# Moving the start addresses of an attention, mixture-of-experts and feed-forward kernel's SBUF pools to multiples of 512 bytes

## The chip, the cores and the metric

The kernel runs on one core of one Trainium2 chip. The metric is the time of the program on the device in microseconds (us), the median of three runs; lower is better. PE is TensorE, DVE is VectorE, ACT is ScalarE, POOL is GpSimd, SP is SyncE, whose queue issues the plain DMAs. SBUF is the memory that the engines read operands from: 128 partitions, in each of which a tile takes a run of bytes. An address below is the byte in a partition at which a tile or a pool of tiles starts.

## The reference, cut to what matters

```python
# q, k, v: (8, 8, 576, 64); attention inside chunks of 64 positions
scores = scale * q_c @ k_c^T; attn = softmax(scores); x = (attn @ v_c) as (4608, 512)
# mixture of experts: 8 experts, each token goes to the one with the largest logit
logits = x @ w_gate; e = argmax(logits); gate = softmax(logits)[e]
x = gate * (relu(x @ w1[e]) @ w2[e])              # w1 512x1024, w2 1024x512
# feed-forward with a rational activation
h = x @ w_in                                      # 512x2048
g = (a0 + a1*h + a2*h^2 + a3*h^3) / (1 + |b0|*|h| + |b1|*h^2 + 1e-6)
return g @ w_out                                  # 2048x512, float64 weights
```

## The kernel before

**Numbers.** Every large product is made from two parts of each operand, a high part in fp32r (the value as TensorE's single-pass format keeps it) and a low part, the rest. `mm3` issues three matmuls for one product: high with high, high with low, low with high (`PASSES`). `split` makes the parts of a weight: ACT copies the raw tile to the high part, DVE (GpSimd for the feed-forward weights that come late) subtracts it for the low part.

**Stages.** First comes attention in 36 tiles of 128 tokens, ordered by hand on PE. It writes x to memory, computes the routing, and sorts tokens into slots. Then come eight experts, each on 512 gathered tokens (the first on 384), ordered by hand on PE, DVE and ACT. `Expert.first(c)` makes 12 matmuls into `h` (stationary: w1, moving: the transposed tokens `xT`), `Expert.second(c)` 12 matmuls into four accumulators `y` (stationary: `hT`, moving: w2). Between them run the extra tiles of 128 tokens (`Extra`, tiles with an `s` or `r` in their names: `hs`, `ys`, `hr`, `yr`), which pass through the same products with their own copies of the weights (`s1`, `s2`) as the moving operand. Last comes the feed-forward in 9 blocks of 512 tokens and 16 chunks c of 128 hidden columns: `first(b, c)` makes the product `f` (stationary: the weights `wf`, moving: `yT`) and the activation on ACT and DVE into `g`; `second(b, c)` makes `z` (stationary: `g`, moving: `wf`). Each is 12 matmuls of 512 columns per chunk. The order inside this last stage is the planner's.

**Where tiles stand.** Pools are laid one after the other from the low end of SBUF in the order in which they are opened; a tile's bytes are rounded up to 32. In front of the first stand 16,384 bytes set aside and four constants of 32. `const` holds small tiles (ident, gate, index tables), 2,976 bytes in all. `xg_p` holds, beside its three buffers of 2,048 bytes, five small tiles of 32 bytes for the extra tiles' indices (`if`, `ix` twice, `ct`, `ce`). Worked out from these sizes:

| pool | what it holds | start before | past a multiple of 512 | start after | past a multiple of 512 |
|---|---|---|---|---|---|
| const | ident and small tables | 16,512 | 128 | 16,512 | 128 |
| ring_a | weights of expert 0, extra tiles' weights, `wf` for c 8 to 15 | 19,488 | 32 | 19,968 | 0 |
| tmp | raw weights, activation's t and u | 85,024 | 32 | 85,504 | 0 |
| xg_p | gathered tokens | 101,408 | 32 | 101,888 | 0 |
| h_p | `hT`, `g` and the extra tiles' `xTs`, `hTs` | 107,712 | 192 | 108,032 | 0 |
| xt_a | `xT`, `yT` of even number | 120,000 | 192 | 120,320 | 0 |
| ring_b | weights of experts 1 to 7, `wf` for c 0 to 7; before it, attention's pools | 136,384 | 192 | 136,704 | 0 |
| xt_b | `xT`, `yT` of odd number | 201,920 | 192 | 202,240 | 0 |
| o_p, cv_p | outputs; conversion of the last weights | 218,304; 222,400 | 192 | 218,624; 222,720 | 0 |

Inside these pools every operand of a 512-column matmul stands a multiple of 512 bytes from its pool's start. Pools opened from the high end (`once`, `rt_p`, `a3_p`) don't move. `ring_b`, `xt_b`, `o_p` and `cv_p` are opened over tiles of earlier stages with `reuse_waits="tile"`: a new tile waits for the old ones whose bytes it takes.

The lines that the text speaks of: L136 and L137 (`split`), L253 (transposes), L259 (`mm3`), L440 to L459 (the activation in `first`), L550 and L569 (attention's q and k).

Of the kernel before, what the change touches and what calls it, by code (L numbers as in the profile page):

```python
# [9 lines left out]
F32 = mybir.dt.float32  # L10
F32R = mybir.dt.float32r
BF16 = mybir.dt.bfloat16
I32 = mybir.dt.int32
U32 = mybir.dt.uint32
# [18 lines left out]
PASSES = ((0, 0), (0, 1), (1, 0))  # L33
CW = 256
CQ = 1.0 + 1e-6
MAN = {mybir.EngineType.PE, mybir.EngineType.DVE, mybir.EngineType.Activation}
SIGN = -0x80000000
EXP_BIAS = 893.0 * 2.0 ** 20
# [3 lines left out]
def kernel(  # L42
# [22 lines left out]
    slots = dram.tile([NE * NT, 1], U32, name="slots")  # L65

    const = ctx.enter_context(tc.tile_pool(name="const", bufs=1))
    ring = {"A": ctx.enter_context(tc.tile_pool(name="ring_a", bufs=8))}
    tmp = ctx.enter_context(tc.tile_pool(name="tmp", bufs=4))

    xg_p = ctx.enter_context(tc.tile_pool(name="xg_p", bufs=3))
# [11 lines left out]
    a3_p = rctx.enter_context(tc.tile_pool(name="a3_p", bufs=2, side="right"))  # L83


    ident = const.tile([128, 128], F32, name="ident")
    make_identity(nc, ident)
    ones = once.tile([128, 128], BF16, name="ones")
    nc.gpsimd.memset(ones, 1.0)
# [32 lines left out]
    cq = const.tile([128, 1], F32, name="cq")  # L122
    nc.vector.memset(cq, CQ)

# [150 lines left out]
    def load_extra(e, nm):  # L275
        r = []
        for src, lab, deint in ((w1r, "w1", True), (w2r, "w2", False)):
            r.append([load_w(extra_src(src, e, c), "A", f"{lab}{nm}_{c}", deint, alternate(c))
                      for c in range(4)])
        return r  # L280

    def expert_of(k_ap):
        return nc.values_load(k_ap, engines=[mybir.EngineType.SP], min_val=0, max_val=NE - 1,
                              skip_runtime_bounds_check_because="one expert's index, or 0, "
                              "out of a table made by comparisons")

    def extra_idx(t, nm):
        m = o_p.tile([128, NE * NOVF], F32, tag="o", name=f"m{nm}")
        V.scalar_tensor_tensor(m, cidx, t[:, 0:1], stf, op0=ALU.is_equal, op1=ALU.mult)
        f = xg_p.tile([128, 2], F32, tag="if", name=f"if{nm}", bufs=1)  # L290
        V.tensor_reduce(f[:, 0:1], m, axis=AX.X, op=ALU.add)
        V.tensor_tensor(out=f[:, 0:1], in0=f[:, 0:1], in1=t[:, 1:2], op=ALU.add)
        V.tensor_scalar(f[:, 1:2], f[:, 0:1], float(NT - 1), None, op0=ALU.min)
        idx = xg_p.tile([128, 2], U32, tag="ix", name=f"ix{nm}", bufs=2)
        V.tensor_copy(idx, f)
        return idx

# [135 lines left out]
    def first(b, c):  # L433
# [13 lines left out]
        last_act = nc.scalar.activation(r, r, AF.Square).ins  # L447
        V.scalar_tensor_tensor(qq, qq, CQ, r, op0=ALU.add, op1=ALU.mult)  # L448
        V.scalar_tensor_tensor(qq, qq, -2.0, r, op0=ALU.add, op1=ALU.mult)  # L449
# [34 lines left out]
    with man:  # L484
# [373 lines left out]
        man.close()  # L858
        man.enter_context(tc.manual_schedule(engines=MAN))

# [65 lines left out]
        def small(name, shape, dt=F32):  # L926
            return rt_p.tile([128] + shape, dt, name=name)
# [44 lines left out]
        ce = small("ce", [NE])  # L972
# [51 lines left out]
        def next_extra(e):  # L1024
            return Extra(extra_idx(tab[:, e], f"s{e}"), (ws1[e], ws2[e]), f"s{e}")
# [223 lines left out]
                               skip_runtime_bounds_check_because="a sum of tile counts over all "  # L1249
                               "tokens, raised to NSTAT, is within these bounds")  # L1250
        with tc.For_i(NSTAT, n_end, 1) as kk:
            ct = xg_p.tile([128, 2], F32, tag="ct", name="ct", bufs=1)
            nc.vector.tensor_copy(ct, tab[:, ds(kk, 1), :].rearrange("p a b -> p (a b)"))
            ce_t = xg_p.tile([1, 1], I32, tag="ce", name="ce_t", bufs=1)
            nc.vector.tensor_copy(ce_t, etab[0:1, ds(kk, 1)])
            ex = Extra(extra_idx(ct, "d"), load_extra(expert_of(ce_t), "d"), "d")
            ex.g()
            ex.x()
            for n in range(2):
                ex.h(n)  # L1260
                ex.r(n)
                ex.t(n)
            for n in range(2):
                ex.y(n)
            ex.out()
# [57 lines left out]
```

## Time and profile before

| what | value |
|---|---|
| median of 3 runs | 1543.64 us (1542.76 to 1545.02) |
| the profiled execution | 1549.44 us, its span 1547.7 us |
| PE busy | 1471.6 us, 95% of the span |
| DVE, ACT, POOL busy | 1284.8, 927.2, 376.8 us |
| granted TensorE clock, mean | 0.990 |

The profile is one execution. Its span is the time from the first to the last instruction. The busy time of PE counts each matmul from its start to its modelled end, and matmuls overlap, so the pace of PE is read from starts: the time from one start to the next. A row that merges n matmuls in the chain of work gives n times that pace; in the timeline a row's length has the last matmul's whole duration in it, so there the pace is taken from the starts of two rows that follow each other.

### The profile page before, as it was taken

What the parts mean: (1) busy time and instruction counts of PE and PEld (TensorE: products, weight loads), DVE (VectorE), ACT (ScalarE), POOL (GpSimd) and SP (SyncE); (2) the same over time, 40 slices, a digit from 0 to 9 for tenths busy, and PEclk for the clock granted to TensorE, in tenths of its full rate; (3) what the DMA queues carried; (4) which work ended last, traced back from release to release, by engine and by line L of the source; (5) the groups of instructions that cost most, each with busy time, mean ns of one, the idle gap of its engine ahead of it and who ended that gap; (6) DMA issues with size and microseconds to landing.
All of it is one profiled execution on the core that took longest, in us unless ns stands there. A gap on an engine that the chain in (4) does not pass through costs nothing.

```text
span 1547.7 us, 22303 instructions
## 1 busy us (share of the span) xinstructions
PE 1471.6 (95%) x7812; PEld 1198.5 (77%) x7812; DVE 1284.8 (83%) x2405; ACT 927.2 (60%) x1456; POOL 376.8 (24%) x307
## 2 busy tenths in 40 slices
PE   6897889999999999997989999999999999999998
PEld 5776678887787777885778888888888888888886
DVE  6787857799889898985989888888888888888886
ACT  5676635454444444444767666666666766766665
POOL 2111122121211212102542222222222222222232
PEclk9999999999999999999999999999999999999999
DMA  8998625777777778663201000010100001000000
GB/s 181 228 251 229 201 84 181 241 248 249 253 233 254 229 232 270 222 214 119 86 28 55 1 28 21 0 48 8 41 14 28 28 1 48 7 35 1 28 1 28
DMA packets 143377, 180.07 MB, mean 116 GB/s; under 512 B 51616, under 2 KB 96672, under 8 KB 143264
## 3 DMA queue, kind: packets, MB, share of 16 engines
q1 hardware_dynamic: 135712, 157.64, 34.1%
q0 software_dynamic: 7552, 21.00, 3.9%
q8 instruction: 62, 1.02, 0.3%
q14 instruction: 51, 0.42, 0.1%
HBM read 140.68 MB, written 37.91 MB: 115 GB/s over the span
## 4 chain that ended last, share of the span: by engine, by line
PE 46%; DVE 3%; issue 2%; POOL 1%; ACT 1%; DMA 0%; SPq 0%; ACTq 0%; POOLq 0%
PE z L259 23%; PE f L259 23%; PE ytp L253 1%; POOL g L459 1%; DVE t L449 1%; POOL wf L137 1%; DVE t L448 0%; DVE t L444 0%; DVE t L450 0%; DMA yg<-ys 0%; DVE t L446 0%; ACT u L445 0%; ACT t L440 0%; DVE yg L718 0%; DVE t L443 0%
## 5 line engine op out<-in xcount | busy, mean ns | idle before, releaser
L259 PE MATMUL f<-yT,wf 128*128 128x512 f32 x1728 | 419.4, 394 | 5.7 <-DVE t L446 2.2
L259 PE MATMUL z<-wf,g 128*128 128x512 f32 x1680 | 411.1, 395 | 9.0 <-ACT g L458 4.6
L259 PEld LDWEIGHTS f<-yT,wf 128*128 128x128 f32 x1728 | 323.5, 188 | 80.5 <-DVE t L446 3.1
L259 PEld LDWEIGHTS z<-wf,g 128*128 128x128 f32 x1680 | 314.6, 189 | 82.1 <-POOL g L459 6.0
L459 POOL TENSOR_TENSOR g<-t,g 128x512 fp32r<-128x512 f32 x140 | 209.6, 1498 | 531.8 <-ACT g L458 501.3
L259 PE MATMUL h<-xT,w 128*128 128x512 f32 (+1 forms) x768 | 184.7, 390 | 6.4 <-DVE hT L379 6.4
L259 PE MATMUL y<-w,hT 128*128 128x512 f32 x744 | 184.0, 396 | 0.0
L443 DVE TENSOR_TENSOR t<-t,f 128x512 f32<-128x512 f32 x144 | 98.6, 685 | 100.6 <-ACT u L442 100.2
L259 PEld LDWEIGHTS h<-xT,w 128*128 128x128 f32 x768 | 144.0, 190 | 35.7 <-DVE hT L379 8.1
L444 DVE SCALAR_TENSOR_TENSOR t<-t,co,u 128x512 f32<-128x512 f32 x144 | 159.1, 1105 | 0.0
L259 PEld LDWEIGHTS y<-w,hT 128*128 128x128 f32 x744 | 136.9, 188 | 28.2 <-issue 0.4
L445 ACT ACTIVATE u<-t,cq 128x512 f32<-128x512 f32 x144 | 104.5, 726 | 85.9 <-DVE t L444 85.3
L458 ACT ACTIVATE g<-t 128x512 fp32r<-128x512 f32 x140 | 89.0, 636 | 99.5 <-DVE t L450 99.5
L440 ACT ACTIVATE t<-f,co 128x512 f32<-128x512 f32 x144 | 112.1, 778 | 49.4 <-PE f L259 34.2
L378 ACT ACTIVATE hT<-h 128x512 fp32r<-128x512 f32 (+1 forms) x64 | 37.5, 585 | 147.0 <-PE h L259 114.1
L450 DVE SCALAR_TENSOR_TENSOR t<-t,co 128x512 f32<-128x512 f32 x144 | 121.8, 846 | 2.0
L448 DVE SCALAR_TENSOR_TENSOR t<-t,u 128x512 f32<-128x512 f32 x144 | 101.9, 708 | 15.5 <-ACT u L447 15.5
L449 DVE SCALAR_TENSOR_TENSOR t<-t,u 128x512 f32<-128x512 f32 x144 | 109.7, 762 | 0.5
L442 ACT ACTIVATE u<-f,co 128x512 f32<-128x512 f32 x144 | 98.3, 683 | 15.0 <-DVE t L449 10.9
L446 DVE SCALAR_TENSOR_TENSOR t<-t,co,f 128x512 f32<-128x512 f32 x144 | 106.2, 738 | 0.0
L447 ACT ACTIVATE u<-u 128x512 f32<-128x512 f32 x144 | 90.4, 628 | 2.2
L441 ACT ACTIVATE t<-f 128x512 f32<-128x512 f32 x144 | 85.1, 591 | 0.0
(203 smaller groups left out, 1951.2 us busy)
## 6 DMA issues: line engine op xcount, KB each, us to landing
raw_w<-in_moe_w_dram SPq DMA_DIRECT2D x64, 512.0 KB
raw_s<-in_moe_w_dram SPq DMA_DIRECT2D x64, 512.0 KB
v<-in_v_dram SPq DMA_DIRECT2D x144, 64.0 KB
xs<-x SPq DMA_DIRECT2D x36, 256.0 KB
out_dram<-o SPq DMA_DIRECT2D x36, 256.0 KB
raw<-in_moe_w_in_dram SPq DMA_DIRECT2D x32, 256.0 KB
raw<-in_moe_w_out_dram SPq DMA_DIRECT2D x32, 256.0 KB
yg<-ys SPq DMA_DIRECT2D x32, 256.0 KB
```

What stands on the lines that cost most here:

```text
L259: nc.tensor.matmul(o, lhsT=lhs(x), rhs=rhs(y), start=(first and n == 0), stop=(last and n == 2))
L440: nc.scalar.activation(p, hp, AF.Identity, scale=a3, bias=a2)
L442: nc.scalar.activation(vv, hp, AF.Abs, scale=b0)
L443: V.tensor_tensor(out=p, in0=p, in1=hp, op=ALU.mult)
L444: V.scalar_tensor_tensor(qq, qq, b1, vv, op0=ALU.mult, op1=ALU.add)
L445: nc.scalar.activation(r, qq, AF.Abs_reciprocal_sqrt, bias=cq)
L446: V.scalar_tensor_tensor(p, p, a1, hp, op0=ALU.add, op1=ALU.mult)
L447: last_act = nc.scalar.activation(r, r, AF.Square).ins
L448: V.scalar_tensor_tensor(qq, qq, CQ, r, op0=ALU.add, op1=ALU.mult)
L449: V.scalar_tensor_tensor(qq, qq, -2.0, r, op0=ALU.add, op1=ALU.mult)
L450: V.scalar_tensor_tensor(p, p, a0, qq, op0=ALU.add, op1=ALU.mult)
L459: nc.gpsimd.tensor_tensor(out=gt[:, 1], in0=p, in1=gt[:, 0].bitcast(F32), op=ALU.subtract)
```

## The change

A new pool `small_p` is opened behind `const` and takes the five small tiles out of `xg_p`. The tile of `ident` gets 80 columns more, which nothing reads. So the tiles that begin behind `const` and `small_p` move up by 480 bytes (`ring_a`, `tmp`, `xg_p`) or 320 bytes (the rest) and begin at multiples of 512. No instruction is added or taken away.

```diff
+PAD = 80
...
     const = ctx.enter_context(tc.tile_pool(name="const", bufs=1))
+    small_p = ctx.enter_context(tc.tile_pool(name="small_p", bufs=1))
     ring = {"A": ctx.enter_context(tc.tile_pool(name="ring_a", bufs=8))}
...
-    ident = const.tile([128, 128], F32, name="ident")
+    ident = const.tile([128, 128 + PAD], F32, name="ident")[:, 0:128]
...
-        f = xg_p.tile([128, 2], F32, tag="if", name=f"if{nm}", bufs=1)
+        f = small_p.tile([128, 2], F32, tag="if", name=f"if{nm}", bufs=1)
...
-        idx = xg_p.tile([128, 2], U32, tag="ix", name=f"ix{nm}", bufs=2)
+        idx = small_p.tile([128, 2], U32, tag="ix", name=f"ix{nm}", bufs=2)
...
-            ct = xg_p.tile([128, 2], F32, tag="ct", name="ct", bufs=1)
+            ct = small_p.tile([128, 2], F32, tag="ct", name="ct", bufs=1)
...
-            ce_t = xg_p.tile([1, 1], I32, tag="ce", name="ce_t", bufs=1)
+            ce_t = small_p.tile([1, 1], I32, tag="ce", name="ce_t", bufs=1)
```

## Rows read from the trace of the kernel before

**Rows 1.** The page's first part: the span, then busy us, share and instructions.
```profile
span 1547.7 us, 22303 instructions
PE 1471.6 (95%) x7812; PEld 1198.5 (77%) x7812; DVE 1284.8 (83%) x2405; ACT 927.2 (60%) x1456; POOL 376.8 (24%) x307
```

**Rows 2.** Windows: busy time and count of each engine by stage, clock, DMA share.
```profile
core 0: us, PE busy (x) PEld busy (x) DVE busy (x) ACT busy (x) POOL busy (x), PEclk, DMA share, GB/s
20.00:160.00 140.00, 118.63 (x1388) 99.77 (x1389) 107.19 (x381) 93.40 (x156) 21.28 (x22) 0.95 0.94 233
280.00:700.00 420.00, 409.55 (x1853) 332.14 (x1852) 377.10 (x775) 191.47 (x249) 75.32 (x65) 0.99 0.75 240
...
840.00:1520.00 680.00, 680.00 (x2995) 554.01 (x2994) 572.97 (x790) 467.65 (x767) 180.72 (x122) 1.00 0.06 19
```

**Rows 3.** The page's chain of work that ended last: shares of the span by engine.
```profile
PE 46%; DVE 3%; issue 2%; POOL 1%; ACT 1%; DMA 0%; SPq 0%; ACTq 0%; POOLq 0%
```

**Rows 4.** Groups of PE's matmuls of 512 columns by tile, with their counts.
```profile
L259 PE MATMUL f<-yT,wf 128*128 128x512 f32 x1728 | 419.4, 394 | 5.7 <-DVE t L446 2.2 <-issue 2.0 <-ACTq L1251 0.9
L259 PE MATMUL z<-wf,g 128*128 128x512 f32 x1680 | 411.1, 395 | 9.0 <-ACT g L458 4.6 <-POOL g L459 4.3
...
L259 PE MATMUL y<-w,hT 128*128 128x512 f32 x744 | 184.0, 396 | 0.0
L259 PE MATMUL h<-xT,w 128*128 128x512 f32 x672 | 166.3, 397 | 6.4 <-DVE hT L379 6.4
...
L259 PE MATMUL ys<-s,hTs 128*128 128x512 f32 x192 | 47.9, 398 | 0.0
L259 PE MATMUL hs<-s,xTs 128*128 128x512 f32 x192 | 47.9, 399 | 0.0
```

**Rows 5.** The chain in order of time, blocks 3 to 5: start, length, matmuls.
```profile
1059.03 5.61 PE z L259 x24
1064.64 5.61 PE f L259 x24
...
1087.05 5.48 PE f L259 x24
...
1098.14 6.16 PE f L259 x27
...
1110.20 0.44 PE ytp L253 x4
...
1138.12 5.48 PE z L259 x24
...
1188.56 6.16 PE f L259 x27
```

**Rows 6.** PE's timeline in the experts' stage: start, length, matmuls merged.
```profile
563.82 2.88 PE L259 MATMUL h<-xT,w 128*128 128x512 f32 x12
566.54 0.60 PE L253 MATMUL xtp<-ident,xg 128*128 128x128 f32 x4
...
573.06 2.98 PE L259 MATMUL hs<-s,xTs 128*128 128x512 f32 x12
575.87 2.92 PE L259 MATMUL y<-w,hT 128*128 128x512 f32 x12
```

**Rows 7.** PE's timeline at expert 0, whose first product has 384 columns.
```profile
235.79 2.25 PE L259 MATMUL h<-xT,w 128*128 128x384 f32 x12
237.88 2.26 PE L259 MATMUL y<-w,hT 128*128 128x512 f32 x9
239.98 2.28 PE L259 MATMUL h<-xT,w 128*128 128x384 f32 x12
```

**Rows 8.** DVE's groups of the low part's subtraction, by ring of the weights.
```profile
L137 DVE TENSOR_TENSOR w<-raw_w,w 128x1024 fp32r<-128x1024 f32 x64 | 78.1, 1220 | 1.7 <-ACT w L136 1.7
L137 DVE TENSOR_TENSOR s<-raw_s,s 128x1024 fp32r<-128x1024 f32 x64 | 77.9, 1218 | 5.5 <-ACT s L136 5.4
```

**Rows 9.** Waits from 20 to 200 us that ended with a load of q or k.
```profile
ACT qkr L550 <- DMA k<-in_k_dram: 9.0, 3, 4.9
```

## The prediction

> **What bounds the kernel now.** I read the page's busy times first. PE is busy for 1471.6 of 1547.7 us, and DVE comes next with 1284.8 [rows 1]. The windows by stage show where that holds: in the feed-forward, from 840 to 1520 us, PE is busy for all of 680 us with 2,995 matmuls, at a granted clock of 1.00, the level of 2.4 GHz; in the experts, from 280 to 700 us, for 409.6 of 420 us. DVE has 573 of 680 and 377 of 420 us there, so it could follow a PE that is a few per cent faster. Attention, from 20 to 160 us, is no PE stage: 118.6 of 140 us, and its DMA engines are at 0.94 [rows 2]. The chain that ended last agrees: of the stretch that it covers nearly all is PE, and DVE, ACT and DMA hold some per cent together [rows 3]. So in the two long stages a nanosecond taken off each matmul comes off the end, and nothing else does.
>
> **What the change does.** It adds, removes and moves no instruction. It changes addresses. The table of pools ahead of this text says which: everything behind the constants goes to a multiple of 512. So I ask whether the trace of before already shows instructions of one shape, in one stage, at different addresses. It does. The feed-forward weights for c 0 to 7 stand in ring_b (192 past a multiple of 512, so a multiple of 64) and those for c 8 to 15 in ring_a (32 past, not a multiple of 64), while `yT` and `g` always stand 192 past. The matmuls of a half differ in nothing else.
>
> **The price of an address on PE.** No matmul of f or z is missing from the trace, so the n-th of the program is the n-th there, and each row of the chain can be told by its chunk. The rows at 1059.03 (z, c 8 and 9) and 1064.64 (f, c 12 to 14) use ring_a: 5.61 / 24 = 233.8 ns from start to start. The rows at 1087.05 and 1098.14 (f, c 0 to 4 of the next block) and at 1138.12 (z, c 6 and 7) use ring_b: 5.48 / 24 = 228.3 and 6.16 / 27 = 228.1 ns [rows 5]. The difference is 5.6 ns, the same for weights that are stationary (f) and for weights that move (z). The experts repeat it: `h`, with w1 from ring_b, goes from 563.82 to 566.54 in 12 matmuls, 226.7 ns each; `hs`, whose weights come from ring_a, from 573.06 to 575.87, 234.2 ns [rows 6]. I take 5.6 ns, the smaller of the two differences. After the change ring_a and its partners stand alike, as ring_b and its partners do today.
>
> One row speaks against so simple a rule. Expert 0's first product has its stationary weights in ring_a too, with 384 columns: from 235.79 to 237.88 is 2.09 us for 12, 174.2 ns each [rows 7]. Against the 226.7 ns of 512 columns in `h` that is 52.5 ns for 128 columns, and 4 x 52.5 = 210, so some 17 ns of each matmul don't go with its columns, in either case: this one seems to pay nothing for its address. I count nothing for these 96.
>
> **How many matmuls gain.** Half of the feed-forward's: of f's 1,728 that is 864, and of z's 1,680 (and 48 more under the name g_last) also 864 [rows 4]. Some of block 0's and of the last block's are covered by ACT and DVE, before 840 us and behind 1515; I take off 88 and keep 1,640. At 5.6 ns they give 9.2 us. In the experts: 192 of `hs` and 192 of `ys` [rows 4], 48 of the first extra tile (hr, yr: 24 each) and 72 of expert 0's second product, whose weights are in ring_a. These are 504, or 2.8 us; with PE at 97.5% there I keep 2.6. The sum is 11.8, so **12 us**. PE's pace there falls by 2.4% in half of the time, and DVE's share rises from 84% to some 86% in the feed-forward, so no other engine becomes the bound.
>
> **What I cost at nothing.** DVE: the subtraction takes 1218 ns when it writes ring_a and 1220 ns when it writes mostly ring_b [rows 8], so phase does not show; bound 0 to 0.2%. Transposes: four of `ytp`, whose source is in xg_p (32 past), take 0.44 us in the chain, 110 ns each [rows 5]; their pace is set by something else or not at all by phase, so I take 0; if 5.6 ns were hidden in each of `ytp`'s 144 (36 tiles of four) it would be 0.8 us. The new pool: the five small tiles keep their numbers of buffers and so their waits. The reused pools: o_p and cv_p now cover 320 bytes more of rt_p's tables, which were last read before those pools open; cover gone, it would be one wait of under a microsecond. DMA: loads of q and k land 192 past a multiple today. The trace doesn't show what an even landing would save, but ACT waits for them for 9.0 us in all [rows 9], so the bounds are 0 and 9; I take 0, since the other engines' shares in attention (DVE 107 of 140 us [rows 2]) close up behind any such gain.
>
> **The rivals.** First, *more than this* (B): even operands at 192 past may pay for not standing at 0. The trace has no large matmul at a multiple of 512, so the bound is the part that doesn't go with the columns, some 17 ns [rows 6, 7], over 5,304 matmuls of 512 columns, 90 us. A quarter of it would be 22 us more: 1510. Against it: the part is the same for 384 columns with other addresses, which looks like a cost of each matmul. The Trainium skill, in "TensorE: Matmul & The Clock Gate", section "Back-to-back issue gap", gives N / 2.4 + 2.5 ns for a warm stream, so 216 ns for 512 columns; by that some 11 ns are open here, but the page says nothing of addresses, and no run here shows 216.
>
> Second, *no change* (C): ring_a's matmuls are slower for where the ring lies, 19 to 85 KB against 136 to 202 KB, or for how far it is from its partner, and 480 bytes alter neither. For it: the 384-column row, which has ring_a and no price. Then the time stays at 1543.6. The Trainium skill, in "SBUF — State Buffer", section "Specifications", speaks for this side: it gives lines of 16 bytes, and every pool of before begins at a multiple of 32, so by it there is nothing to straighten. The trace doesn't agree with that as the whole story: 233.8 against 228.1 ns [rows 5].
>
> Third, *slower* (D): all streams of PE and of ACT begin at one phase and collide. The place is ring_b's matmuls, 864 + 864 + 672 of h and 672 of y, 3,072; the price, if they all fall to 233.8 ns, is 17 us, with nothing gained on ring_a: 1561. It decides from the point at which ring_b's rows pass 231 ns. Against it: today both operands of these matmuls are at one phase, 192, and they are the fast ones.
>
> **How the numbers follow.** The profiled execution took 1549.44 us, 5.8 over the median, span and 1.7 us around it; the difference of 12 us is taken from the median: 1543.6 - 12 = 1531.6, and a profile of about 1537. Chances: this case 0.64, with its own range 1526 to 1538 (5.6 ns could be 3 to 8); B 0.16; C 0.13; D and a planner's order that comes out worse 0.07. Below 1526 is B; I hold its small half, to 1506, inside. Upwards the range goes to 1541, where the gain would be lost in what a measurement of this kernel can tell from no change, 0.2% or 3.1 us. So 1506 to 1541. Faster is this case and B, 0.80; same is C, 0.13; slower 0.07.
>
> **What would show it.** Right: chain rows of 24 matmuls at 5.44 to 5.50 us in both halves of a block, `hs` and `ys` at 227 to 229 ns, a block of the feed-forward of some 89.3 us where it is 90.4 (1098.14 to 1188.56 [rows 5]), and DVE's durations as they were. B would show as rows under 5.40 us in ring_b's half. C would show as rows of 5.61 left where ring_a is read; D as rows of 5.6 where ring_b is. If attention ends some microseconds earlier, the landing of DMAs counts after all. The prediction is wrong if the pace depends on something other than the phase of the two operands, or if the planner orders the feed-forward differently once addresses change.

## The result, and the profile after

The kernel after takes 1529.22 us (median of 4 runs, 1525.02 to 1529.83), the kernel before, measured beside it, 1544.33 us (4 runs, 1542.76 to 1547.04): a ratio of 0.9895, with a 95% interval of 0.9872 to 0.9917. That is 16 us less (0.0105 x 1544), with an interval of 13 to 20. The profiled execution of after took 1525.02 us, the fastest of its four; that of before [rows 1], 1549.44 us, lay 5.1 us over the median just given. So the spans differ by 24.4 us, more than the medians do, and sums below are set against the ratio.

The page's first part, after (it answers [rows 1]):
```profile
span 1523.3 us, 22302 instructions
PE 1454.1 (95%) x7812; PEld 1198.0 (79%) x7812; DVE 1285.5 (84%) x2405; ACT 923.8 (61%) x1456; POOL 376.8 (25%) x307
```
PE has the same 7,812 matmuls and is busy 17.5 us less; DVE's time has not moved. Every engine's instructions stand in the order of before, but for two neighbouring matmuls of attention, so places in the two traces can be matched one to one. All lines behind the constants are 4 further down: L259 is now L263.

The groups by tile, PE's matmuls h and f, give where the stages begin (min, median, max duration, then first and last start). Before:
```profile
L259 PE MATMUL h<-xT,w x768: 335/389/632, 217.6 to 685.3; 128*128 128x512 f32 x168, 128*128 128x384 f32 x24
L259 PE MATMUL f<-yT,wf x1728: 387/393/505, 710.8 to 1527.3; 128*128 128x512 f32 x192
```
After:
```profile
L263 PE MATMUL h<-xT,w x768: 333/389/792, 204.4 to 672.7; 128*128 128x512 f32 x168, 128*128 128x384 f32 x24
L263 PE MATMUL f<-yT,wf x1728: 387/389/628, 697.6 to 1502.8; 128*128 128x512 f32 x192
```
Attention, up to the first h, takes 217.6 and then 204.4 us (13.2 less in these two executions, which differ more than the medians; their granted clock differed there too, 0.88 from 20 to 60 us before and 0.96 after). The experts, from the first h to the first f, take 493.2 and 493.2. The feed-forward, from the first f to the span's end, takes 836.9 and then 825.7: 11.2 us less.

The chain in order of time, after, for one block (it answers [rows 5]; start, length, matmuls):
```profile
1080.27 6.12 PE f L263 x27
...
1088.66 3.40 PE z L263 x15
...
1097.09 2.72 PE z L263 x12
...
1120.11 5.44 PE z L263 x24
1125.55 5.67 PE f L263 x25
1131.22 5.44 PE z L263 x24
1136.66 5.44 PE f L263 x24
...
1169.30 6.12 PE f L263 x27
```
The rows that read ring_a (1131.22, z; 1136.66, f) and those that read ring_b (1120.11) have one pace now: 5.44 / 24 = 226.7 ns. The block goes from 1080.27 to 1169.30, 89.03 us where it was 90.42.

Two more rows of before, from the same view, show what I had not read there:
```profile
1106.57 3.40 PE z L259 x15
...
1114.99 2.72 PE z L259 x12
```
These use ring_b too and already ran at 3.40 / 15 = 226.7 ns. The ring_b rows of [rows 5], 228 ns, each stand right behind a run that read ring_a, and their first matmuls still carry its cost.

The experts' timeline after (it answers [rows 6]):
```profile
560.42 2.88 PE L263 MATMUL hs<-s,xTs 128*128 128x512 f32 x12
563.14 2.89 PE L263 MATMUL y<-w,hT 128*128 128x512 f32 x12
```
From start to start, `hs` takes 2.72 / 12 = 226.7 ns; it was 234.2. Yet the stage is no shorter. The waits of PE in its 487 us (engine, line, what it waited for, us in total, times, longest) show where this went; before, from 223 to 710 us, and after, from 210 to 697:
```profile
PE h L259 <- DVE hT L379: 6.4, 4, 1.8
```
```profile
PE h L263 <- DVE hT L383: 8.9, 4, 2.6
```
The windows of the same two stretches (us, PE busy, PEld, DVE, ACT, POOL, clock, DMA share, GB/s):
```profile
223.00:710.00 487.00, 475.13 (x2197) 387.03 (x2195) 421.83 (x886) 223.32 (x296) 93.22 (x81) 0.99 0.72 230
```
```profile
210.00:697.00 487.00, 472.14 (x2195) 386.82 (x2195) 421.40 (x885) 223.06 (x297) 93.50 (x81) 0.99 0.72 230
```
PE's busy time fell by 3.0 us, and 2.5 us of it came back as a longer wait for `hT` from DVE.

In attention the DMA engines are less busy for what they move. Windows from 60 to 140 us, before and after:
```profile
60.00:140.00 80.00, 71.27 (x855) 59.69 (x851) 66.17 (x240) 56.40 (x94) 15.32 (x16) 0.98 0.96 251
```
```profile
60.00:140.00 80.00, 69.62 (x847) 59.45 (x845) 67.48 (x247) 57.68 (x96) 13.42 (x14) 0.98 0.88 245
```
They moved 251 / 0.96 = 261 GB/s for each unit of busy share before, and 245 / 0.88 = 278 after.

### The profile page after: what moved, and what is told of

Its sections match the earlier page's. It is cut to its first block, busy times and chain, and to the rows that moved or that the text cites. A ratio compares the mean times of both kernels' runs of the same rounds, so it can differ in the third digit from the quotient of the medians.

```text
span 1523.3 us, 22302 instructions
## 1 busy us (share of the span) xinstructions
PE 1454.1 (95%) x7812; PEld 1198.0 (79%) x7812; DVE 1285.5 (84%) x2405; ACT 923.8 (61%) x1456; POOL 376.8 (25%) x307
## 5 line engine op out<-in xcount | busy, mean ns | idle before, releaser
L263 PE MATMUL f<-yT,wf 128*128 128x512 f32 x1728 | 414.6, 392 | 5.7 <-DVE t L450 2.2
L263 PE MATMUL z<-wf,g 128*128 128x512 f32 x1680 | 405.7, 392 | 7.7 <-POOL g L463 4.8
L263 PEld LDWEIGHTS f<-yT,wf 128*128 128x128 f32 x1728 | 324.3, 188 | 75.0 <-DVE t L450 3.1
L263 PEld LDWEIGHTS z<-wf,g 128*128 128x128 f32 x1680 | 314.5, 188 | 75.8 <-POOL g L463 6.7
L263 PE MATMUL h<-xT,w 128*128 128x512 f32 (+1 forms) x768 | 184.7, 390 | 8.9 <-DVE hT L383 8.9
L263 PE MATMUL y<-w,hT 128*128 128x512 f32 x744 | 183.9, 395 | 0.0
L447 DVE TENSOR_TENSOR t<-t,f 128x512 f32<-128x512 f32 x144 | 98.5, 684 | 90.4 <-ACT u L446 89.8
L263 PEld LDWEIGHTS h<-xT,w 128*128 128x128 f32 x768 | 144.2, 191 | 38.0 <-DVE hT L383 10.8
L263 PEld LDWEIGHTS y<-w,hT 128*128 128x128 f32 x744 | 136.9, 188 | 27.9 <-issue 0.4
L444 ACT ACTIVATE t<-f,co 128x512 f32<-128x512 f32 x144 | 112.0, 778 | 33.6 <-PE f L263 17.5
```

The source lines that it names most:

```text
L263: nc.tensor.matmul(o, lhsT=lhs(x), rhs=rhs(y), start=(first and n == 0), stop=(last and n == 2))
L444: nc.scalar.activation(p, hp, AF.Identity, scale=a3, bias=a2)
L447: V.tensor_tensor(out=p, in0=p, in1=hp, op=ALU.mult)
```

## The experiments

**The questions.** My theory was that the two operands of a matmul must stand at one phase, whichever it is, so that their distance decides. Its rival: each operand must by itself begin at a round address. A second pair is about attention: are its loads cheaper for where they land, or is the difference only one between two executions? A third: what swallowed the experts' gain? In the table, "distance" is that of ring_a from the operands that its matmuls are paired with, "landing" is where attention's tiles begin past a multiple of 512, the row is a chain row of 24 matmuls of z that read ring_a, the block goes from the first f of block 4 to that of block 5, and the last column is GB/s over DMA share from 60 to 140 us, as above. Ratios are against the kernel before in the same set of runs (its medians in the three sets: 1545.29, 1552.08 and 1544.79 us).

| kernel | distance | landing | row, us | block, us | ratio, 95% interval | GB/s over share |
|---|---|---|---|---|---|---|
| before | 160 | 192 | 5.61 | 90.4 | 1 | 261 |
| after | 0 | 0 | 5.44 | 89.0 | 0.9895 (0.9872 to 0.9917) | 278 |
| all32 | 0 | 32 | 5.44 | 89.0 | 0.9925 (0.9900 to 0.9950) | 261 |
| all64 | 0 | 64 | 5.44 | 89.0 | 0.9937 (0.9911 to 0.9962) | 266 |
| ringA32 | 32 | 0 | 5.60 | 90.3 | 0.9959 (0.9944 to 0.9975) | 283 |
| tmp32 | 0 | 0 | 5.44 | 89.0 | 0.9878 (0.9853 to 0.9904) | 283 |
| attn192 | 0 | 192 | 5.44 | 89.0 | 0.9927 (0.9909 to 0.9945) | 268 |
| attn0 | 160 | 0 | 5.61 | 90.4 | 0.9969 (0.9954 to 0.9983) | 281 |
| rest64 | 64 | 64 | 5.59 | 90.0 | 0.9976 (0.9962 to 0.9991) | 267 |
| rest128 | 128 | 128 | 5.58 | 90.2 | 0.9977 (0.9963 to 0.9991) | 267 |
| rest256 | 256 | 256 | 5.44 | 89.0 | 0.9910 (0.9887 to 0.9933) | 285 |

**all32 and all64: every pool off the round addresses, all alike.**
```diff
-PAD = 80
+PAD = 88
```
(all64: `PAD = 96`.)

> The changed kernel with 32 bytes more in front: every pool behind the constants begins 32 past a multiple of 512, so the two operands of each matmul stand alike, but neither at a multiple of 64. Theory 1 (each operand has to begin at a multiple of 64): all rows of 24 matmuls at 5.6 us, a block of the feed-forward of some 91.5 us, slower than before, some 1548 to 1558. Theory 2 (only the distance between the two operands counts): rows of 5.44 us as in the changed kernel, a block of 89.0, some 1529.

> The changed kernel with 64 bytes more in front: every pool behind the constants begins 64 past a multiple of 512. Theories 1 and 2: as the changed kernel, rows of 5.44 us, a block of 89.0, some 1529. Theory 3 (a multiple of 128 or more is needed): rows of 5.5 us and more, a block over 89.6.

The chain of all32, rows that read ring_a:
```profile
1047.08 5.44 PE z L263 x24
1052.52 5.44 PE f L263 x24
```
With every operand 32 past a multiple of 512, which was ring_a's own place in the kernel before, all matmuls run at 226.7 ns. So 32 was never a bad address: the theory that each operand must begin at a round one falls, and the distance of the two is what counts. Both kernels are slower than after all the same, by a ratio of 0.003 to 0.004 (a small difference: the intervals overlap), with their feed-forward as short; that pointed to attention.

**ringA32 and tmp32: one part of the change undone.**
```diff
-PAD = 80
+PAD = 0
...
+    ring = {"A": ctx.enter_context(tc.tile_pool(name="ring_a", bufs=8))}
     small_p = ctx.enter_context(tc.tile_pool(name="small_p", bufs=1))
-    ring = {"A": ctx.enter_context(tc.tile_pool(name="ring_a", bufs=8))}
+    gap_p = ctx.enter_context(tc.tile_pool(name="gap_p", bufs=1))
+    gap = gap_p.tile([128, 80], F32, name="gap")
+    nc.gpsimd.memset(gap, 0.0)
```
This is ringA32: `small_p` and the gap stand behind ring_a, so ring_a alone is at 32 again. In tmp32 they stand behind tmp, so the raw weights and the activation's t and u are at 32 (`total` moves to a pool of its own behind ring_a).

> The changed kernel with ring_a alone put back to 32 past a multiple of 512, all other pools at 0. Theories 1 and 2: the rows that read ring_a go back to 5.61 us, those that read ring_b keep 5.44; a block of some 90.2; 9 to 11 us over the changed kernel. If ring_a's phase is not what counted: 89.0 and some 1529.

> The changed kernel with tmp alone (raw weights, the activation's t and u, which ACT and DVE read and write) put back to 32 past a multiple of 512, all pools of matmul operands at 0. If tmp's phase slowed some matmuls of ring_b's half in the kernel before (228.2 where the changed kernel has 226.7 ns): rows of 5.48 us in both halves, a block of 89.4 to 89.6, 2 to 4 us over the changed kernel. If only the operands' own phase counts: 89.0 and some 1529.

The chain of ringA32:
```profile
1051.26 5.60 PE z L266 x24
1056.85 5.60 PE f L266 x24
...
1079.22 5.48 PE f L266 x24
```
With ring_a alone back, 233.3 ns return to its rows and 90.3 us to the block, and the ring_b row behind them (1079.22) is 5.48 again. For tmp, which PE never reads, the phase did not show in the time.

**attn192 and attn0: the two halves of the gain, apart.**
```diff
+        gap_p = actx.enter_context(tc.tile_pool(name="gap_p", bufs=1))
+        gap = gap_p.tile([128, 48], F32, name="gap")
+        nc.gpsimd.memset(gap, 0.0)
         qk_p = actx.enter_context(tc.tile_pool(name="qk_p", bufs=2))
```
This is attn192, made from after; attn0 is the same with 80 columns, made from before.

> The kernel after, with a tile of 192 bytes that nothing reads in front of attention's pools, so that q, k, v and their copies stand 192 past a multiple of 512 as they did before; the feed-forward's and the experts' pools stay at 0. Theory L (the loads of q and k go faster into tiles that begin at a multiple of 512): attention gets some 5 us longer, the DMA share from 60 to 140 us goes from .84 and .92 back to .93 and .99, and the time is 1533 to 1536, with a feed-forward block of 89.0 us as in the kernel after. Theory M (all of the gain is matmuls): 1527 to 1530 and DMA shares as after.

> The kernel before, with a tile of 320 bytes that nothing reads in front of attention's pools, so that these alone begin at a multiple of 512; the rings and everything of the experts and the feed-forward stand as before. Theory L: attention is some 5 us shorter and the time is 1537 to 1541, with ring_a's matmuls at 234 ns and a block of 90.4 us. Theory M: 1543 to 1546.

The windows from 60 to 140 us, attn192 and then attn0:
```profile
60.00:140.00 80.00, 70.25 (x859) 59.52 (x855) 67.43 (x245) 58.48 (x98) 14.85 (x16) 1.00 0.94 252
```
```profile
60.00:140.00 80.00, 69.55 (x860) 58.88 (x861) 68.00 (x252) 58.60 (x97) 13.44 (x14) 1.00 0.88 247
```
The matmuls alone give 0.9927, or 11.3 us of 1552 (interval 8.5 to 14.1); attention's addresses alone give 0.9969, or 4.8 us (2.6 to 7.1). Multiplied they are 0.9896, and the whole change measured 0.9895. Nothing else is needed. The absolute times that I had expected were missed by 2.7 and 5.6 us at their upper ends, and attn0's 1546.6 us taken alone would speak for theory M; but the kernel before was itself slower in this set (1552.08), and the ratios are what was asked.

The traces hold each DMA packet with its size and time, and they say more of which transfers gain. From 20 to 150 us the packets of 512 bytes are those of q and k: they take 32.9 to 34.9 ns in the mean in each of the seven kernels whose tiles land off a multiple of 256 (lean_before, below, is one), and 30.2 to 30.4 ns in each of the seven others. Those of 256 bytes (v) go from 20.2 to 20.9 down to 19.0 to 19.4, those of 2,048 (the stores of x) from 95.8 to 98.9 down to 90.6 to 92.5. The length of attention in one execution is no such measure: up to the first h it is 206.6 to 217.6 us in the first seven and 200.9 to 214.5 in the others.

**rest64, rest128 and rest256: how far apart is alike.**
```diff
     ring = {"A": ctx.enter_context(tc.tile_pool(name="ring_a", bufs=8))}
+    gap_p = ctx.enter_context(tc.tile_pool(name="gap_p", bufs=1))
+    gap = gap_p.tile([128, 16], F32, name="gap")
+    nc.gpsimd.memset(gap, 0.0)
```
(16 columns are 64 bytes; 32 and 64 columns for the other two.)

> The kernel after, with 64 bytes between ring_a and the pools behind it: ring_a at 0, all others 64 past a multiple of 512, so ring_a's matmuls have operands 64 apart, ring_b's have them alike. Theory P64 (what counts is the distance of the two operands within 64 bytes): all matmuls at 227 ns, a block of 89.0 us, time as with all pools at 64, 1533 to 1536. Theory P512 (the two must stand alike within 512): ring_a's matmuls at 230 to 234 ns, a block of 89.6 to 90.4 us, time 1536 to 1546.

> The kernel after, with 128 bytes between ring_a and the pools behind it: ring_a at 0, all others 128 past a multiple of 512. Period 256 (the distance must be a multiple of 256): ring_a's matmuls at 230 to 234 ns, a block of 89.9 to 90.4 us, as at a distance of 64. Period 128: all matmuls at 227 ns and a block of 89.0 us. The loads of q and k land 128 past: attention's DMA shares as with all pools at 64 (above .90 from 100 to 140 us) if only multiples of 256 help them, as in the kernel after if 128 does.

> The kernel after, with 256 bytes between ring_a and the pools behind it: ring_a at 0, all others 256 past a multiple of 512. Theory P64 or a period of 256: all matmuls at 227 ns, a block of 89.0 us; theory P512: ring_a's matmuls at 230 to 234 ns and a block of 89.6 to 90.4 us. The loads of q and k land at 256: if a multiple of 256 is enough for them, attention is as in the kernel after and the time with all matmuls at 227 ns is 1527 to 1530; if it must be 512, 1533 to 1536.

The chains of rest64, rest128 and rest256, rows of z and then f that read ring_a:
```profile
1051.51 5.73 PE f L266 x25
1057.23 5.59 PE z L266 x24
1062.83 5.59 PE f L266 x24
```
```profile
1047.75 5.58 PE z L266 x24
1053.33 5.58 PE f L266 x24
```
```profile
1050.23 5.44 PE z L266 x24
1055.67 5.44 PE f L266 x24
```
In the rows of z, distances of 64 and 128 bytes cost as much as 32 and 160 do, within 1.3 ns a matmul (5.58 to 5.61 us for 24), and 256 costs nothing. In f the cost at 64 is smaller in some rows: the 25 matmuls of c 10 to 12, all from ring_a, take 5.73 us there, 229.2 ns each. In after the same 25 take 5.67 us, and in before:
```profile
1143.60 5.85 PE f L259 x25
```
The whole feed-forward agrees. From the first f to the span's end it takes 825.4 to 826.3 us in every kernel with a distance of 0 or 256, 833.6 at 64, 834.7 at 128 and 836.4 to 836.9 at 32 and 160. So of the distances tried, 32, 64, 128 and 160 pay and 0 and 256 don't: a period of 256 bytes, not the 64 that I had favoured. Landing has the same period. The window of rest256:
```profile
60.00:140.00 80.00, 70.01 (x868) 58.74 (x864) 68.48 (x256) 57.66 (x95) 14.34 (x15) 1.00 0.87 248
```
285 GB/s over share, where 32, 64, 128 and 192 past a multiple of 256 give 261 to 268. The time alone doesn't settle this: 1535.48 us is what I had expected if it must be 512, and the ratio's interval holds after's 0.9895 as well as attn192's 0.9927. The rate and the packets (30.4 ns for 512 bytes) put rest256 with after.

**lean_before and lean_after: DVE taken out of the experts' way.**
```diff
-        V.tensor_scalar(t, high, 0x7ff00000, None, op0=ALU.bitwise_and)
...
+        V.tensor_scalar(t, high, 0x7fffffff, None, op0=ALU.bitwise_and)
...
-            V.tensor_tensor(out=tf, in0=highf, in1=lowf, op=ALU.add)
             nc.sync.dma_start(dst, tf)
```

> The kernel before, with the conversion of the last weights cut from eight DVE instructions per piece to one, so some 2.5 us per piece leave DVE in the experts' stage; the feed-forward then computes with weights that aren't the real ones. It is the partner of the next run. Theory A (in the experts' stage DVE's work sets the pace and swallows what PE gains): PE's waits for hT from DVE (6.4 us before) fall to under 3 us, and the stage, 493 us from the first matmul of expert 0 to the first of the feed-forward, gets shorter, to some 485 us. Rival A2 (the stage's length is set by DMA, the outputs that are still being scattered): the waits of DVE for that stay at 17 us or grow, and the stage stays at 492 to 494 us.

> The same cut in the kernel after. Theory A: with DVE out of the way the 504 matmuls' 2.6 to 3.0 us come off the end: the experts' stage is 2 to 3 us shorter than in the run before, and the two kernels' medians differ by 18 to 19 us, where the uncut ones differ by 15 to 16. Rival A2: the two stages are equal within 1 us and the medians differ by 15 to 16 us.

The groups by tile of lean_before, then of lean_after, and the windows of their stages, in the same order:
```profile
L250 PE MATMUL h<-xT,w x768: 335/389/481, 211.9 to 663.1; 128*128 128x512 f32 x168, 128*128 128x384 f32 x24
L250 PE MATMUL f<-yT,wf x1728: 387/393/628, 688.0 to 1504.1; 128*128 128x512 f32 x192
```
```profile
L254 PE MATMUL h<-xT,w x768: 331/389/486, 207.9 to 657.0; 128*128 128x512 f32 x168, 128*128 128x384 f32 x24
L254 PE MATMUL f<-yT,wf x1728: 387/389/796, 682.4 to 1487.9; 128*128 128x512 f32 x192
```
```profile
212.00:688.00 476.00, 473.99 (x2243) 390.39 (x2243) 279.62 (x453) 223.16 (x302) 97.80 (x83) 1.00 0.71 236
```
```profile
208.00:682.00 474.00, 471.48 (x2243) 390.37 (x2243) 279.78 (x452) 222.42 (x302) 97.79 (x83) 1.00 0.71 237
```
Without that work the stage falls from 493.2 to 476.1 us (I had expected 485), PE's waits for `hT` in front of `h` are gone, and PE is busy for all but 2 us. DVE's waits for the outputs still being scattered stay at 18.9 and 22.1 us, so they were not what set the pace: rival A2 falls. Now the change does shorten the stage: 476.1 to 474.5, 1.6 us, with PE's busy time down by 2.5. That is under the 2 to 3 that I expected, and it comes from single executions: among the twelve kernels that keep the work, the stage scatters from 492.5 to 496.1 us. The direction is what the theory asked for; the size is not shown. The medians are 1529.06 and 1508.43 us, 0.9907 (0.9886 to 0.9927) and 0.9769 (0.9749 to 0.9788) of before. Their difference of 20.6 us is no sharper test: the two intervals leave it some 4 us either way, and the uncut pair's is 13 to 20.

**ident0: the transposes' operands alike.**
```diff
+    tab = const.tile([128, NOVF, 2], F32, name="tab")
+    etab = const.tile([128, NOVF], I32, name="etab")
     ident = const.tile([128, 128 + PAD], F32, name="ident")[:, 0:128]
```

> The kernel after, with two tables moved in front of the tile of ident, so that this begins at a multiple of 512 (16,896) and not 128 past one, as every transpose's other operand does from then on. If the distance of the two operands costs transposes too (5 to 6 ns each, over 144 of ytp in the feed-forward's chain and some 500 in attention, most of them hidden), the time falls by 1 to 3 us against the kernel after, to a ratio of 0.988; if it doesn't, the ratio is the kernel after's, 0.9895, and four ytp take 0.44 us in the chain as before.

1526.62 us, a ratio of 0.9883 (0.9864 to 0.9903): not to be told from after's. Its chain:
```profile
1106.45 0.44 PE ytp L259 x4
```
Four transposes take 0.44 us with ident at 0, as with ident at 128. No version tried is faster than after by more than the measurement can tell; tmp32 and ident0 overlap with it.

## Why the prediction came out as it did

**The whole.** 1531.6 us was predicted and 1529.22 measured; by difference, 12 and 16 us. The case that was held likeliest came in. That the sum came so near is in part luck: the feed-forward was put 2.0 us too low and the experts 2.6 us too high, which cancel, so that the miss which is left is about attention's 4.8 us. The terms, one by one:

**FFN, 9.2 us.** Measured 11.2. The mechanism was right (attn192 carries it alone, ringA32 takes it back); the price of 5.6 ns was too small. The step that failed: "I take 5.6 ns, the smaller of the two differences". The pace of ring_b was read from chain rows that follow a run of ring_a's, 228.2 ns; rows further from one stood in the same chain at 226.7, as did `h` in [rows 6]. 233.8 - 226.7 = 7.1 ns, and 7.1 x 1,640 = 11.6. The chain shows it without any model, too: from the row of 27 f to the z row of c 6 and 7, where 137 of 167 matmuls read ring_b, a block took 1138.12 - 1098.14 = 39.98 us before and 1120.11 - 1080.27 = 39.84 after; the rest of it, mostly ring_a, 50.44 and 49.19.

**Experts, 2.6 us.** Measured 0 (493.2 and 493.2). One pair of executions can't show that alone, but the others agree: the stage takes 493.7 us in the mean of the seven kernels with a distance of 0 or 256, and 493.9 in the mean of the five others. The matmuls did get faster, by 7.5 ns in `hs`, and PE's work there by 3.0 us, more than I had put down. What failed is the step "with PE at 97.5% there I keep 2.6": it took a busy share for a proof that PE sets the pace. DVE set it at those places where PE waited for `hT`, and the prediction's own [rows 2] had DVE at 90% of that stage. So the sentence that DVE "could follow a PE that is a few per cent faster" fails in the experts. The lean pair shows that DVE's work held the stage (17 us went with it); that some of PE's gain then comes through, 1.6 us, is seen in one pair of executions only.

**Expert 0's 96 of 384 columns, 0.** In after the 12 go from 222.67 to 224.78, 175.8 ns each, where it was 174.2 [rows 7]: no gain, as taken, and I still can't say why they don't pay.

**Attention's loads, bounds 0 and 9, taken 0.** Measured 4.8 (attn0). The bounds held and the value did not. The step "I take 0, since the other engines' shares in attention [...] close up behind any such gain" failed: DMA was at 0.94 to 0.96, the busiest of all there. The one visible wait, ACT for k, was a poor guide: it went from 9.0 only to 7.4 us in after. The Trainium skill, in "DMA: Bandwidth & Descriptors", section "How a descriptor splits into AXI transactions", says that a transaction must start at a multiple of 256 bytes and that a descriptor which doesn't start there pays for bytes outside it. The page tells it of reads, and the tiles of q, k and v are addresses written to; in period it agrees with the runs (256 as good as 0; 32, 64, 128 and 192 not). The prediction had not weighed that rule, and by the table of pools no large load of before lands in a tile at a multiple of 256.

**Costs taken at nothing.** DVE's duration of the subtraction, 1219 and 1217 ns after against [rows 8], transposes (ident0) and tmp (tmp32) don't show the phase, as taken.

**The rivals.** B (even pairs pay too) falls: at 0 as at 32, 64, 192 and 256 an even pair goes at 226.7 ns. What the prediction held against it, that the 17 ns are the same for 384 columns, was no evidence: they had been worked out from the rows of 512 and 384 columns on the premise that both have them. Its 216 ns "for a warm stream" need a correction too: the Trainium skill, in "TensorE: Matmul & The Clock Gate", section "Back-to-back issue gap", calls that formula the gap of a single, isolated matmul. The large matmuls of all runs here go at 226.7 ns at best. C falls with ringA32. D falls: ring_b's rows of 24 are at 5.44 us in after.

**The reason behind it.** That the pools begin at a multiple of 512 is more than PE needs: its gain comes from equal distance, which all32 has as well. For the loads a multiple of 256 is enough. The weight loads show nothing of it: PEld is busy for 1198.5 us before and 1198.0 after. What in the chip makes a pair of operands at different places within 256 bytes slower was not found; the runs show only when it happens and what it costs.

## What to carry to other kernels

When two instructions of one shape run at two paces, sort them by the addresses of their operands before looking for a wait, and read the fast pace from rows that stand far from slow ones. In this kernel it was worth 0.7% to give both operands of each large fp32r matmul the same place within 256 bytes, and 0.3% to let a transfer-bound stage's loads land at a multiple of 256. A busy share of 97% doesn't make an engine the one that sets the pace: the few waits in the stage, and how busy the engine that ends them is, decide whether a gain comes through.

## What was not expected of the hardware

- A 512-column fp32r matmul takes 226.7 ns from start to start where its two operands stand alike within 256 bytes, and some 232 to 234 where they stand 32, 128 or 160 bytes apart, whether ring_a gives the stationary operand (f) or the moving one (z). At 64 bytes it is 233 in z, and from 229 to 233 in f.
- The cost lingers: a ring_b run right behind a ring_a run took 5.48 us for 24 matmuls instead of 5.44, with nothing wrong in its own addresses. In z of c 6 [rows 5, 1138.12] the first eight starts are 224 to 236 ns apart, and the rest 226 to 227. A tail of up to ten such steps also stands behind the transposes of `ytp`, in after and even in ident0, where their operands stand alike, so it follows other breaks too.
- Loads into SBUF in attention: 278 to 285 GB/s over DMA share where the tiles begin at a multiple of 256, 261 to 268 elsewhere. The packets of q and k gain most, by some 10%, those of v and of x's stores by 6%; the tiles of q, k, v and x were not moved apart from each other.
